# Attention and routed experts on one core: experts with up to 192 tokens get a short branch in which both parts of x pass a weight together

## The chip, the cores and the metric

The kernel runs on one core of a Trainium2 chip. The metric is the device time of one execution in microseconds; the time before is the median of three runs. The profile is one execution taken by the hardware profiler.

## The reference, cut to what matters

First an attention layer: 8 batches, 8 heads, 512 local and 32 global positions, head size 64; local positions attend to a window of 32 on either side and to the global ones, global positions to all. Its output is read as `x`, 4608 tokens of 512. Then a mixture of experts in float32:

```python
do_compute = x @ w_skip > 0
out = x.copy()
xc = x[do_compute]
logits = xc @ w_gate                       # 8 experts
e_idx = np.argmax(logits, axis=1)
gate_w = softmax(logits)[e_idx]
for e in range(8):
    mask = e_idx == e
    h = np.maximum(xc[mask] @ w1[e], 0.0)  # w1: 512 x 1024
    y[mask] = gate_w[mask] * (h @ w2[e])   # w2: 1024 x 512
out[do_compute] = xc + y
```

With the inputs of seed 0 the reference sends 1980 tokens to experts, by expert 395, 171, 153, 289, 173, 371, 253 and 175. The work of each expert depends on its count.

## The kernel before, in words

**Attention and routing** fill the first half. The rows of `out` are written as they come, the router's lists of tokens are scattered into `lst` in DRAM, one list per expert, and the weights of expert 0 are loaded and split alongside.

**The experts** run one after the other from line 969. A group is 256 tokens (`GRP`), in two tiles of 128. GpSimd gathers an expert's first group from `out` into `xfirst` or `xsecond` in turn, and the second group, tokens 256 to 511, into `xmore`; rows beyond the list's end are not moved. `turn_x` (line 832) transposes a group on TensorE and splits it into a rounded part `xh` and the rest `xl`, since TensorE works on rounded float32 (`F32R`). Weights are split likewise: `Weights.split` (line 175) has ScalarE copy a raw chunk of 128 x 1024 to the high part (line 181), and VectorE subtract for the low part (line 184). An expert has eight such chunks of 512 KB, loaded by SP into a ring of six raw buffers (`load`, line 159). The chunks of the next expert are split while the present one computes; the split weights lie in two sets of tiles in turn.

**One group** is done by `ffn` (line 848). The first pass makes the hidden layer in eight blocks f of 128: twelve matmuls of 128 x 256 into one bank `ph` (line 858), four for each of w1h·xh, w1l·xh and w1h·xl; then ScalarE writes the rounded, rectified `hh` (line 863) and VectorE the rest `hlw` (line 864). Three banks serve `ph` in turn. The second pass makes an output tile of 128 tokens by 24 matmuls of 512 columns into `py` (line 874), three for each f: hh·w2h, hh·w2l, hlw·w2h. It runs twice, for t = 0 and 1. `put` (line 936) has VectorE multiply by the gate and add x (line 939), into a buffer `yo` (a pool of two) or `ylast` (one), and GpSimd scatter the rows into `out` (line 940).

**The order of the work around this** is written by hand. All engines record under a manual schedule. `hook(i)` is called behind each block of the first pass (i = 0 to 7), behind each f of the first output tile (8 to 15), and of the second (16 to 23). The table `todo` hangs on it: splits of the next expert's chunks at 0, 1, 2, 4, 5, 6, 9 and 11, and at 16 `nxt`, which loads the expert's count into a register of each engine and turns the next expert's x (`xt`, line 837). Expert 1 also splits the last four chunks of its own weights, at 0 to 3.

**More than 256 tokens** are handled behind the first group under `tc.If(num > GRP)` (line 1010): up to 128 more by `ffn_half` (line 890), otherwise by a further `ffn`. The scatter of the first group's second tile (`leave()`, line 1031) comes last. Each engine tests its own register and jumps.

Of the kernel before, what the change touches and what calls it, by code (L numbers as in the profile page):

```python
# [19 lines left out]
P = 128  # L20
# [14 lines left out]
CAP = NT  # L35
# [4 lines left out]
NSUB = GRP // P  # L40


@with_exitstack
def kernel(
# [59 lines left out]
    def slots(es, g):  # L104
        if g == 0:
            nc.sync.dma_start(
                lt[:, es, 0].rearrange("p e t c -> p e (t c)"),
                l3[es, 0:GRP, :].rearrange("e (p t) c -> p e (t c)", t=NSUB),
            )
        else:  # L110
            for t in range(NSUB):
                nc.sync.dma_start(
                    lt[:, es, 1, t],
                    l3[es, GRP + t * P:GRP + (t + 1) * P, :].rearrange("e p c -> p e c"),
                )
# [22 lines left out]
    wq = {}  # L138

    WC = 1024  # L140

    class Weights:


        def __init__(self, e, pool):
# [5 lines left out]
            self.loaded, self.done, self.n = 0, 0, 2 * NC * F // WC  # L151
# [7 lines left out]
        def load(self, eng=nc.sync):  # L159
            if self.loaded < self.n:  # L160
                i, self.loaded = self.loaded, self.loaded + 1
                raw = self.raw[i] = stage.tile([P, WC], F32, tag="raw", name="raw")
                j = i % (self.n // 2)
                if i < self.n // 2:
                    eng.dma_start(raw, w1[self.e, j * P:(j + 1) * P, :])
                else:
                    k = WC // DM
                    eng.dma_start(
                        raw.rearrange("p (c n) -> p c n", n=DM),
                        w2[self.e, j * k * P:(j + 1) * k * P, :].rearrange(  # L170
                            "(c p) n -> p c n", p=P
                        ),
                    )

        def split(self, eng, parts=1, later=None):
            if self.done < parts * self.n:
# [3 lines left out]
                hi, lo, raw = self.view(i, "h")[:, sl], self.view(i, "l")[:, sl], self.raw[i][:, sl]  # L180
# [639 lines left out]
    stage = ctx.enter_context(tc.tile_pool(name="stage2", bufs=6))  # L820
# [7 lines left out]
    xs = [  # L828
        [f1.tile([P, NC, GRP], F32R, name=f"x{part}{i}") for part in "hl"] for i in range(2)
    ]  # L830

    def turn_x(xg, i, nt=NSUB):
        xh, xl = xs[i]
# [12 lines left out]
        return xh, xl  # L846

    def ffn(e, x2, xg, gate, sidx, hook=lambda i: None, bank=ps_t):
        hl = wq[e]
        xh, xl = x2  # L850
        hh = fw.tile([P, NF, GRP], F32R, name="hh", bufs=1)
        hlw = fw.tile([P, NF, GRP], F32R, name="hlw", bufs=1)
        for f in range(NF):
            ph = ps_s("ph") if bank is ps_v else bank("ph")
            i = 0
            for a, bb in (("w1h", xh), ("w1l", xh), ("w1h", xl)):
                for c in range(NC):
                    nc.tensor.matmul(  # L858
                        ph[:, 0:GRP], hl[a][:, c, f * P:(f + 1) * P], bb[:, c, :],
# [8 lines left out]
            hook(f)  # L868
        for t in range(NSUB):
            py = bank("py")  # L870
            ts_ = slice(t * P, (t + 1) * P)
            for f in range(NF):
                for i, (a, bb) in enumerate(((hh, "w2h"), (hh, "w2l"), (hlw, "w2h"))):
                    nc.tensor.matmul(  # L874
                        py, a[:, f, ts_], hl[bb][:, f, :],
                        start=f == 0 and i == 0, stop=f == NF - 1 and i == 2,
                    )
                hook(NF * (t + 1) + f)

            def leave(t=t, py=py):  # L880
                yo = None
                if t and bank is ps_v:
                    yo = fw.tile([P, DM], F32, name="ylast", bufs=1)
                put(py, gate(t), xg[:, t, :], sidx[:, t:t + 1], yo)

            if t == 0:
                leave()
        return leave

    def ffn_half(e, x2, xg, gate, sidx):  # L890

        hl = wq[e]
        xh, xl = x2
        hh = fw.tile([P, NF, GRP], F32R, name="hh", bufs=1)
# [51 lines left out]
    with tc.manual_schedule(engines=engines | {mybir.EngineType.SP}):  # L946
# [14 lines left out]
        def rest():  # L961
# [4 lines left out]
            for _ in range(4):  # L966
                weights[1].load(nc.gpsimd)
# [126 lines left out]
```

## Time and profile before

| | us |
|---|---|
| median of three runs | 499.26 (497.95 to 500.41) |
| the profiled execution | 503.73 |
| its span, first to last instruction | 502.0 |
| first matmul of expert 0's first pass | 247.6 |
| first matmul of expert 1 | 298.29 |
| first matmul of expert 7 | 469.53 |
| last matmul ends | 491.67 |

The mean granted clock of TensorE is 0.986. HBM traffic is 194 GB/s over the span.

A row of a timeline has start, duration, engine, line, operation, output and inputs, shape, count, and in brackets the idle time of the engine before it with what ended it. PE is TensorE's matmul, PEld its weight load, DVE VectorE, ACT ScalarE, POOL GpSimd, SP the queue that issues most DMAs. A matmul's own duration holds its latency: matmuls overlap, and their pace is read from start to start. A group's row ends in busy time and mean ns of one, and idle time before.

### The profile page before, as it was taken

The page shows a single profiled execution, that of the slowest core. Times are in us where ns is not written, and L with a number is a line of the kernel's source. Part 1 is how long each engine was busy: PE and PEld are TensorE (multiplying, and loading weights), DVE is VectorE, ACT ScalarE, POOL GpSimd, SP SyncE. Part 2 cuts the span into 40 slices and gives each one's busy share as a digit, 9 for nine tenths or more (in the row PEclk, how much of TensorE's full clock was granted, in tenths as well). Part 3 has the DMA queues.
Part 4 walks back from the last instruction along what each step waited for, and adds up shares of the span by engine and source line. Part 5 has one row for each costly group of instructions (what it writes and reads, how often), then busy time and mean ns, then how long its engine had stood idle before and what let it go on. Part 6 is the DMA issues. An engine that isn't in the chain of part 4 may idle for free. (4 is left out here: it accounts for less than half of the span.)

```text
span 502.0 us, 13663 instructions
## 1 busy us (share of the span) xinstructions
PE 455.9 (91%) x4962; PEld 368.5 (73%) x4962; DVE 298.7 (59%) x1221; ACT 289.6 (58%) x883; POOL 228.2 (45%) x236
## 2 busy tenths in 40 slices
PE   8799999999989998887698999999989999899991
PEld 3576767776666767666696979898968888688881
DVE  6886767877757767784453229684714757047310
ACT  4689999899868887764341208563514545145210
POOL 6656666669864677776246014323202341013300
PEclk9999999999999999999899999999999999899996
DMA  8899898889957788610547308883820949113100
GB/s 252 267 329 262 268 288 279 254 281 219 289 171 244 226 189 255 169 45 2 172 146 216 109 26 268 313 295 121 286 99 10 343 142 327 38 23 131 46 15 17
DMA packets 50545, 93.32 MB, mean 186 GB/s; under 512 B 15596, under 2 KB 19948, under 8 KB 50448
## 3 DMA queue, kind: packets, MB, share of 16 engines
q1 hardware_dynamic: 44624, 81.83, 52.0%
q0 software_dynamic: 5824, 10.25, 6.2%
q8 instruction: 55, 0.90, 0.9%
q14 instruction: 42, 0.34, 0.3%
HBM read 82.91 MB, written 14.67 MB: 194 GB/s over the span
## 5 line engine op out<-in xcount | busy, mean ns | idle before, releaser
L368 ACT ACTIVATE prob<-prob,nmx 128x160 f32<-128x160 f32 x256 | 106.4, 418 | 17.9 <-DVE nmx L363 15.7
L398 POOL TENSOR_TENSOR prob<-prob,inv 128x640 f32<-128x640 f32 x64 | 80.3, 1257 | 61.1 <-DVE ing L428 24.0
L863 ACT ACTIVATE hh<-ph 128x256 fp32r<-128x256 f32 x72 | 27.7, 385 | 83.2 <-PE ph L858 71.8
L940 POOL DMA_INDIRECT out_dram<-yo,six x12 | 12.2, 1018 | 134.6 <-DVE yo L939 116.7
L874 PE MATMUL py<-w2h,hh 128*128 128x512 f32 x144 | 57.2, 397 | 0.0
L874 PE MATMUL py<-w2h,hlw 128*128 128x512 f32 x144 | 56.9, 395 | 0.0
L874 PE MATMUL py<-w2l,hh 128*128 128x512 f32 x144 | 56.7, 394 | 0.0
L351 PE MATMUL pss<-ks,qs 64*64 64x160 f32 x1024 | 51.5, 305 | 3.1 <-DVE nmx L363 1.6
L864 DVE SCALAR_TENSOR_TENSOR hlw<-ph,hh 128x256 fp32r<-128x256 f32 x72 | 30.3, 421 | 32.4 <-ACT hh L863 29.6
L351 PEld LDWEIGHTS pss<-ks,qs 64*64 64x64 f32 x1024 | 34.1, 134 | 20.9 <-issue 15.2
L858 PE MATMUL ph<-xh,w1h 128*128 128x256 f32 x288 | 46.4, 283 | 3.2 <-ACT xh L844 1.5
L482 PEld LDWEIGHTS pv<-ptT,vw 128*64 128x64 f32 x1024 | 39.4, 137 | 13.3 <-issue 3.9
L368 ACT ACTIVATION_READ_ACCUMULATOR prob<-prob,nmx 128x1 f32 x256 | 48.4, 189 | 0.0
L482 PE MATMUL pv<-ptT,vw 128*64 128x64 f32 (+1 forms) x1024 | 44.2, 237 | 3.4 <-ACT ptT L441 1.6
L858 PE MATMUL ph<-xh,w1l 128*128 128x256 f32 x288 | 45.5, 280 | 0.0
L858 PE MATMUL ph<-xl,w1h 128*128 128x256 f32 x288 | 45.4, 280 | 0.0
L858 PEld LDWEIGHTS ph<-xh,w1h 128*128 128x128 f32 x288 | 39.3, 191 | 5.9 <-issue 3.8
L639 POOL DMA_INDIRECT lst<-dat,slu x34 | 34.3, 1008 | 18.0 <-DVE cni L959 9.6
L858 PEld LDWEIGHTS ph<-xh,w1l 128*128 128x128 f32 x288 | 39.1, 190 | 0.0
L858 PEld LDWEIGHTS ph<-xl,w1h 128*128 128x128 f32 x288 | 39.0, 190 | 0.0
L438 PE MATMUL pst<-ident,prob 128*128 128x128 f32 x256 | 36.6, 281 | 2.5 <-POOL prob L398 1.2
L184 DVE TENSOR_TENSOR w1l<-raw,w1h 128x1024 fp32r<-128x1024 f32 x28 | 34.1, 1220 | 6.6 <-ACT w1h L181 4.1
(178 smaller groups left out, 942.3 us busy)
## 6 DMA issues: line engine op xcount, KB each, us to landing
raw<-in_w_dram SPq DMA_DIRECT2D x60, 512.0 KB
vw<-in_v_dram SPq DMA_DIRECT2D x32, 512.0 KB
ks<-in_kT_dram SPq DMA_DIRECT2D x32, 400.0 KB
out_dram<-xr SPq DMA_DIRECT2D x32, 256.0 KB
qs<-in_qT_dram SPq DMA_DIRECT2D x31, 256.0 KB
vgs<-in_vgl_dram SPq DMA_DIRECT2D x32, 64.0 KB
raw<-in_w_dram POOLq DMA_DIRECT2D x4, 512.0 KB
lst<-dat,slu POOLq DMA_INDIRECT x34
```

The costliest lines, as they stand in the source:

```text
L184: eng.tensor_sub(lo, raw, hi.bitcast(F32))
L351: nc.tensor.matmul(banks[odd][head(h ^ odd), j * W:(j + 1) * W], q[head(h), w * QB:(w + 1) * QB], window(k[head(h)], w), start=True, stop= ...
L368: nc.scalar.activation(pt[:, i, :], pt[:, i, :], AF.Exp, bias=nmx[:, i:i + 1], scale=-1.0, accum_out=sums[:, i, 0:1],)
L398: nc.gpsimd.tensor_mul(pt[:, sl, :], pt[:, sl, :], inv[:, sl].unsqueeze(2).to_broadcast([P, 4, W]),)
L438: nc.tensor.transpose(pst[:, i * P:(i + 1) * P], pt[:, 4 * hf + i, 0:KW], ident)
L482: nc.tensor.matmul(pv[head(h), j * 96:j * 96 + n], vv[:, w, head(h)], ptT[:, w, h ^ odd, 0:n], start=j == 0, stop=False, skip_group_check= ...
L639: ins = nc.gpsimd.indirect_dma_start(out=lst, out_offset=bass.IndirectOffsetOnAxis(ap=slu[:, t:t + 1], axis=0), in_=dat[:, bs[j], t - 4 * ...
L858: nc.tensor.matmul(ph[:, 0:GRP], hl[a][:, c, f * P:(f + 1) * P], bb[:, c, :], start=i == 0, stop=i == 3 * NC - 1,)
L863: nc.scalar.activation(hh[:, f, :], ph[:, 0:GRP], AF.Relu)
L864: nc.vector.scalar_tensor_tensor(hlw[:, f, :], ph[:, 0:GRP], 0.0, hh[:, f, :].bitcast(F32), ALU.max, ALU.subtract,)
L874: nc.tensor.matmul(py, a[:, f, ts_], hl[bb][:, f, :], start=f == 0 and i == 0, stop=f == NF - 1 and i == 2,)
L940: ins = nc.gpsimd.indirect_dma_start(out=out, out_offset=bass.IndirectOffsetOnAxis(ap=sidx, axis=0), in_=yo, in_offset=None, bounds_check= ...
```

## The change

For experts 1 to 7 the first pass and the second output tile stand in an If with two branches each, on whether the count is over 192 (`FEW`, 128 + 64).

- **The long branch** (`up`, `down`) computes as before, and holds the work on more than 256 tokens (`more`) and the second tile's scatter from `ylast`.
- **The short branch of the first pass** (`up_few`): the two parts of x lie in one tile, so that 2 x 192 columns pass a w1h chunk in one matmul of 384 columns; w1l takes 192 columns of the high part. The bank then holds the high sum beside w1h·xl. ScalarE copies the second half into a `yo` buffer, VectorE adds the first, ScalarE rectifies, VectorE subtracts. The last two follow one block later.
- **The short branch of the second output tile** (`down_few`): `hh` and `hlw` are now one tile `h2`. GpSimd copies the low parts of the last 64 tokens into the columns behind their high parts. Sixteen matmuls with these 128 columns against w2h and w2l make upper and lower halves of `py`, which `leave_few` adds: ScalarE copies the lower half to `ylast`, VectorE takes two steps into a `yo` buffer, and GpSimd scatters 64 rows.
- In the short branch every fourth chunk's subtraction (the third of eight; in expert 1 also the seventh of its own) that falls into the first pass is GpSimd's.
- The first output tile stands between the two Ifs, outside of them.
- `nxt` moves from 16 to 15, ahead of the second If, and loads the next expert's count; expert 1's last splits are at 13 and 14 instead of 13 and 15.
- Weight loads: the raw buffers are six fixed tiles, and SP issues a load behind each split, across experts (`feed`), instead of all eight at the expert's start.
- The lists of experts 1 to 7 are loaded by tile (tokens 0 to 127, then 128 to 255), by two DMAs instead of one, so that tokens 128 to 191 are the first half of the second tile.
- The order of the weights' and x's arithmetic in the long branch, `ffn` for further groups and `ffn_half` stay.

```diff
+Q = P // 2
+FEW = P + Q
...
-        if g == 0:
+        if g == 0 and es.start == 0:
...
-                raw = self.raw[i] = stage.tile([P, WC], F32, tag="raw", name="raw")
...
+                raw = raws[(NCH * (self.e - 1) + i) % len(raws)] if raws else self.raw[i]
...
+    raws.extend(stage.tile([P, WC], F32, name=f"raw{i}") for i in range(6))
...
+    xs = [f1.tile([P, 2, NC, GRP], F32R, name=f"x{i}") for i in range(2)]
+    h2 = f1.tile([P, 2, NF, GRP], F32R, name="h2")
+    hh, hlw = h2[:, 0], h2[:, 1]
...
+    def up_few(e, x2, hook, bank):
+
+        hl, late = wq[e], []
+        for f in range(NF):
+            ph = bank("ph")
+            fs = slice(f * P, (f + 1) * P)
+            for c in range(NC):
+                nc.tensor.matmul(
+                    ph[:, 0:2 * FEW], hl["w1h"][:, c, fs], x2[:, :, c, 0:FEW],
+                    start=c == 0, stop=False, skip_group_check=True,
+                )
+            for c in range(NC):
+                nc.tensor.matmul(
+                    ph[:, 0:FEW], hl["w1l"][:, c, fs], x2[:, 0, c, 0:FEW],
+                    start=False, stop=c == NC - 1, skip_group_check=True,
+                )
+            hs = fw.tile([P, DM], F32, name="yo")[:, 0:FEW]
+            nc.scalar.copy(hs, ph[:, FEW:2 * FEW])
+            nc.vector.tensor_add(hs, ph[:, 0:FEW], hs)
+            if late:
+                late.pop()()
+
+            def part(f=f, hs=hs):
+                h, lo = hh[:, f, 0:FEW], hlw[:, f, 0:FEW]
+                nc.scalar.activation(h, hs, AF.Relu)
+                nc.vector.scalar_tensor_tensor(
+                    lo, hs, 0.0, h.bitcast(F32), ALU.max, ALU.subtract
+                )
+
+            late.append(part)
+            if f == NF - 1:
+                late.pop()()
+            hook(f)
...
+    def down_few(e, hook, bank):
+
+        hl = wq[e]
+        py = bank("py")
+        for f in range(NF):
+            for i, bb in enumerate(("w2h", "w2l")):
+                nc.tensor.matmul(
+                    py, hh[:, f, P:GRP], hl[bb][:, f, :],
+                    start=f == 0 and i == 0, stop=f == NF - 1 and i == 1,
+                )
+            hook(2 * NF + f)
+        return py
...
+    def leave_few(py, xg, gate, sidx):
+        ys = fw.tile([P, DM], F32, name="ylast", bufs=1)
+        nc.scalar.copy(ys[0:Q], py[Q:P])
+        put(py, gate(1), xg[:, 1, :], sidx[:, 1:2], None, ys)
...
-                for _ in range(8 if e else 4):
-                    weights[e + 1].load()
+                for _ in range((4, 2, 0)[min(e, 2)]):
+                    feed()
...
+                    w.split(nc.gpsimd if few and w.done % 4 == 2 else nc.vector)
+                    if e:
+                        feed()
...
+                with tc.If(nums[e] > FEW) as many:
+                    up(e, xs[e % 2], hook, ps_s)
...
+                with many.Else():
+                    up_few(e, xs[e % 2], hook, ps_s)
+                    nc.gpsimd.tensor_copy(hh[:, :, FEW:GRP], hlw[:, :, P:FEW])
+                few = False
+            put(down(e, 0, hook, ps_v), gate(0), xg[:, 0, :], sidx[:, 0:1])
+            if e == 0:
+                second()
+            else:
+                with tc.If(nums[e] > FEW) as many:
+                    second()
+                with many.Else():
+                    leave_few(down_few(e, hook, ps_v), xg, gate, sidx)
```

More of the change, by code (lines that the diff above doesn't have):

```diff
@@ L868, in ffn @@
             hook(f)
-        for t in range(NSUB):
[L870 to L887, printed above, removed]
@@ new lines, in down @@
+    def down(e, t, hook, bank):
+        hl = wq[e]
+        py = bank("py")
+        ts_ = slice(t * P, (t + 1) * P)
+        for f in range(NF):
+            for i, (a, bb) in enumerate(((hh, "w2h"), (hh, "w2l"), (hlw, "w2h"))):
+                nc.tensor.matmul(
+                    py, a[:, f, ts_], hl[bb][:, f, :],
+                    start=f == 0 and i == 0, stop=f == NF - 1 and i == 2,
+                )
+            hook(NF * (t + 1) + f)
+        return py
+    def down_few(e, hook, bank):
+        hl = wq[e]
+        py = bank("py")
+        for f in range(NF):
+            for i, bb in enumerate(("w2h", "w2l")):
+                nc.tensor.matmul(
+                    py, hh[:, f, P:GRP], hl[bb][:, f, :],
+                    start=f == 0 and i == 0, stop=f == NF - 1 and i == 1,
+                )
+            hook(2 * NF + f)
+        return py
@@ L895, in ffn_half @@
-        hlw = fw.tile([P, NF, GRP], F32R, name="hlw", bufs=1)
+        xh, xl = x2[:, 0], x2[:, 1]
         hr = []
@@ L1031, with hook, gate, second @@
-            leave()
-            x2 = x2n[0] if x2n else None
+                todo[15] = nxt
+            def hook(i):
+                todo.get(i, int)()
+            def gate(t):
+                return lt[:, e, 0, t, 1:2]
+            sidx = six[:, e, 0, :]
+            def second():
+                py = down(e, 1, hook, ps_v)
+                with tc.If(nums[e] > GRP):
+                    more(e, nums[e])
+                yl = fw.tile([P, DM], F32, name="ylast", bufs=1)
+                put(py, gate(1), xg[:, 1, :], sidx[:, 1:2], yl)
@@ new lines @@
+            few = False
+            if e == 0:
+                up(e, xs[0], hook, ps_s)
+            else:
+                kept, fed0 = [(w, w.done) for w in weights.values()], fed[0]
+                with tc.If(nums[e] > FEW) as many:
+                    up(e, xs[e % 2], hook, ps_s)
+                for w, w.done in kept:
+                    pass
+                few, fed[0] = True, fed0
+                with many.Else():
+                    up_few(e, xs[e % 2], hook, ps_s)
+                    nc.gpsimd.tensor_copy(hh[:, :, FEW:GRP], hlw[:, :, P:FEW])
+                few = False
```

149 lines of the change are left out of this document (77 added, 72 removed).

## The prediction, made before the run

> **What bounds the kernel now.** I read the page's first part, the busy time of each expert's stretch, and then the timelines of TensorE, ScalarE, VectorE and GpSimd at the seams between experts. The experts are counted from 0; by the token counts given above 1, 2, 4 and 7 have at most 192 tokens; I call them few-experts. First the page (busy us, share, count), then the stretches of experts 1 to 7, each from its first matmul to that of the next (width, then busy us of PE, PEld, DVE, ACT, POOL, then PE clock, DMA share, GB/s).
>
> ```profile
> PE 455.9 (91%) x4962; PEld 368.5 (73%) x4962; DVE 298.7 (59%) x1221; ACT 289.6 (58%) x883; POOL 228.2 (45%) x236
> ```
> ```profile
> 298.29:322.12 23.83, 23.54 (x152) 21.11 (x153) 19.59 (x25) 15.75 (x22) 7.97 (x7) 1.00 0.77 268
> 322.12:345.77 23.65, 23.50 (x152) 20.97 (x153) 14.75 (x21) 11.66 (x18) 7.14 (x6) 1.00 0.70 249
> 345.77:383.18 37.41, 36.01 (x213) 30.83 (x214) 16.86 (x23) 14.26 (x24) 6.98 (x6) 1.00 0.41 137
> 383.18:406.76 23.58, 23.43 (x153) 20.89 (x152) 15.76 (x22) 11.57 (x18) 7.69 (x7) 1.00 0.65 225
> 406.76:445.95 39.19, 37.59 (x212) 31.96 (x213) 16.86 (x23) 14.27 (x24) 6.98 (x6) 0.96 0.41 140
> 445.95:469.53 23.58, 23.43 (x154) 20.90 (x152) 15.67 (x22) 11.45 (x18) 7.10 (x7) 1.00 0.31 95
> 469.53:492.00 22.47, 22.14 (x144) 19.82 (x144) 5.08 (x11) 3.07 (x8) 4.08 (x4) 1.00 0.07 22
> ```
>
> TensorE is busy in all but 0.1 to 1.6 us of each stretch, at full clock: matmuls bound these experts, and a matmul removed is time removed, as long as nothing else becomes late. VectorE is second, with 15 to 20 of 24 us. TensorE's rhythm and two seams without more tokens (expert 1 to 2, and 2 to 3), then the seam behind expert 0, where two jumps follow each other:
>
> ```profile
> 321.43 0.40 PE L874 MATMUL py<-w2h,hlw 128*128 128x512 f32 x1
> 322.12 0.71 PE L858 MATMUL ph<-xh,w1h 128*128 128x256 f32 x4 [0.29 <-PEq L1010]
> ...
> 323.14 0.63 PE L858 MATMUL ph<-xl,w1h 128*128 128x256 f32 x4
> 323.60 0.63 PE L858 MATMUL ph<-xh,w1h 128*128 128x256 f32 x4
> ...
> 339.47 0.39 PE L874 MATMUL py<-w2h,hlw 128*128 128x512 f32 x1
> 339.70 1.04 PE L837 MATMUL xt<-ident,xsecond 128*128 128x128 f32 x8
> 340.49 0.48 PE L874 MATMUL py<-w2h,hh 128*128 128x512 f32 x1
> ...
> 345.23 0.40 PE L874 MATMUL py<-w2h,hlw 128*128 128x512 f32 x1
> 345.77 0.72 PE L858 MATMUL ph<-xh,w1h 128*128 128x256 f32 x4
> ```
> ```profile
> 296.92 0.40 PE L874 MATMUL py<-w2h,hlw 128*128 128x512 f32 x1
> 298.29 0.71 PE L858 MATMUL ph<-xh,w1h 128*128 128x256 f32 x4 [0.97 <-PEq L1016]
> ```
>
> Start to start, four 256-column matmuls take 0.46 to 0.47 us (0.117 each) and one of 512 columns 0.23: 0.456 ns a column. One jump costs 321.43 to 322.12 less 0.23 = 0.46 us, or 0.31 in the last pair of the first fence; I take 0.4. Two in a row cost 296.92 to 298.29 less 0.23 = 1.14.
>
> **The change, part by part.** (1) The first pass of a few-expert. On TensorE, the last output block of a first pass and the start of the second pass, before and after (xh and xl are the parts of x, h_4459 the joint tile of both parts of h):
>
> ```order
> L858 MATMUL ph<-xh_4451,w1h 128x256 x4
> L858 MATMUL ph<-xh_4451,w1l 128x256 x4
> L858 MATMUL ph<-xl_4452,w1h 128x256 x4
> L874 MATMUL py<-w2h,hh 128x512
> L874 MATMUL py<-w2l,hh 128x512
> ```
> ```order
> L883 MATMUL ph<-x_4458,w1h 128x384 x4
> L888 MATMUL ph<-x_4458,w1l 128x192 x4
> L1128 UNCONDITIONAL_BRANCH
> L916 MATMUL py<-w2h,h_4459 128x512
> L916 MATMUL py<-w2l,h_4459 128x512
> ```
>
> In each of eight blocks, twelve matmuls of 256 columns became four of 384 and four of 192. Before: 96 x 0.117 = 11.2 us. After, by columns: 32 x 0.175 + 32 x 0.0875 = 8.4 us. The 192-column ones may not reach 0.0875, since each loads 128 fresh weight columns: the eight transposes above, with 128 moving columns, take 0.79 us, 0.099 each, not 0.058. By that row the pass is 8.8 us; I take 8.8. [...]
>
> (2) The second output tile has 16 instead of 24 matmuls: 5.6 to 3.7 us. TensorE alone then needs 8.8 + 5.6 + 0.8 (transposes) + 3.7 + two jumps of 0.4 = 19.7 us for expert 1, 2 or 4, some 4.0 less than before. For expert 7, which turns no next x, it is 18.5 up to its last matmul, instead of 22.0 (469.53 to 491.5).
>
> (3) ScalarE and VectorE get more to do per block, and the first copy waits for something new. ScalarE at the start of expert 2, before and after (DMASW numbers are the counters of GpSimd's indirect DMAs, gathers and scatters):
>
> ```order
> L863 ACTIVATE hh<-ph 128x256 [waits DVE_49,PE_49,Activation_49]
> L181 CAST w1h<-raw 128x1024 [waits DMAHW1_49]
> L863 ACTIVATE hh<-ph 128x256 [waits PE_49]
> L181 CAST w1h<-raw 128x1024 [waits DMAHW2_49]
> L863 ACTIVATE hh<-ph 128x256 [waits PE_49]
> ```
> ```order
> L893 COPY yo<-ph 128x192 [waits DMASW2_49,DMASW4_49,DMASW1_49,DMASW5_49,DVE_49,DMASW6_49,PE_49,Activation_49]
> L188 CAST w1h<-raw_4451 128x1024 [waits DMAHW1_49]
> L893 COPY yo<-ph 128x192 [waits DMASW4_49,DMASW2_49,DMASW6_49,PE_49,Activation_49]
> L900 ACTIVATE h_4459<-yo 128x192 [waits DVE_49]
> L188 CAST w1h<-raw_4452 128x1024 [waits DMAHW2_49]
> ```
>
> The copy lands in a yo buffer, one of two from which outputs are scattered. So it waits until the last scatter of the expert before has landed. Behind it on ScalarE wait the casts, behind them VectorE's subtractions, and TensorE, with three banks for ph, stops at its fourth block. The prices, from VectorE and ScalarE in expert 2, and from GpSimd at the seams behind experts 0 and 3:
>
> ```profile
> 325.20 1.23 DVE L184 TENSOR_TENSOR w1l<-raw,w1h 128x1024 fp32r<-128x1024 f32 x1 [0.51 <-issue]
> 326.35 0.42 DVE L864 SCALAR_TENSOR_TENSOR hlw<-ph,hh 128x256 fp32r<-128x256 f32 x1
> 326.68 1.22 DVE L184 TENSOR_TENSOR w1l<-raw,w1h 128x1024 fp32r<-128x1024 f32 x1
> ```
> ```profile
> 325.48 1.04 ACT L181 CAST w1h<-raw 128x1024 fp32r<-128x1024 f32 x1
> ```
> ```profile
> 298.38 0.97 POOL L940 DMA_INDIRECT out_dram<-yo,six  x1 [4.51 <-DVEq L1016]
> 300.69 0.97 POOL L940 DMA_INDIRECT out_dram<-ylast,six  x1 [1.33 <-DMA out_dram<-yo,six]
> ...
> 384.47 1.00 POOL L940 DMA_INDIRECT out_dram<-yo,six  x1 [19.96 <-DVE yo L939]
> ```
>
> A weight subtraction holds VectorE 1.15 us, a 256-column step 0.33. I estimate 0.27 for each of the two 192-column steps (by length). A scatter lands about 2.2 us after its start (298.38 to just before 300.69). VectorE has 5 subtractions (the third goes to GpSimd) and 16 short steps in the pass: 5.7 + 4.3 = 10 us. With the first copy and cast ahead of it (0.35 + 1.04) and one more such pair where VectorE runs dry behind the blocks without a subtraction of its own, the last h is ready 12.8 us after the first copy, an estimate from these rows. The end of the expert is then 0.7 + 0.8 + 0.4 + 3.7 later: 18.4 us after the first copy, plus 0.4 to the next, 18.8. The copy can start 1.3 us in at the earliest (a block takes 1.1), and each us beyond is lost.
>
> When can it start? Ahead of expert 2 stands a few-expert. Its end is a copy on ScalarE of half an output, priced by the whole ones in the group below (0.57), two VectorE steps of 0.75 (the row of 491.71 further down), and a scatter:
>
> ```profile
> L549 ACT COPY xr<-pr 128x512 f32<-128x512 f32 x28 | 15.7, 568 | 0.0
> ```
>
> That is 0.8 with the wait for TensorE, + 1.5 + 0.2 + 2.2 = 4.7 us after the last matmul, 4.3 after expert 2 begins. Behind expert 0: 300.6, about 1.6 after a start at 299.0. Behind expert 3: 384.47 + 2.2, 2.4 after a start at 384.3. Behind expert 6 (no more tokens, last yo scatter long landed): no wait.
>
> (4) GpSimd takes one subtraction (two in expert 1) and the copy of h. SP's next weight load waits for that subtraction, and so do all loads behind it.
>
> ```profile
> L184 POOL TENSOR_TENSOR w2l<-raw,w2h 128x512 fp32r<-128x512 f32 x8 | 10.2, 1279 | 0.0
> ```
> ```profile
> 301.96 1.58 POOL L119 DMA_INDIRECT xmore<-out_dram,six  x1 [0.31 <-issue]
> ...
> 306.72 1.16 POOL L119 DMA_INDIRECT xfirst<-out_dram,six  x1 [0.30 <-issue]
> ```
>
> GpSimd's queue at the start of expert 4, before and after:
>
> ```order
> L119 DMA xmore<-out_dram,six 128x512 x2
> L119 DMA xsecond<-out_dram,six 128x512 x2
> L940 DMA out_dram<-yo,six 4352x512
> L982 TENSOR_LOAD cni
> L1010 COMPARE_AND_BRANCH
> ```
> ```order
> L121 DMA xmore<-out_dram,six 128x512 x2
> L121 DMA xsecond<-out_dram,six 128x512 x2
> L1128 COMPARE_AND_BRANCH
> L1128 UNCONDITIONAL_BRANCH
> L191 TENSOR_TENSOR w1l<-raw_4451,w1h 128x1024
> L1135 COPY h_4459<-h_4459 128x8x64
> ```
>
> The subtraction stands behind the four gathers, which end 9.6 us into expert 1, and takes 2 x 1.28 = 2.6. The late casts of expert 1 therefore wait for loads issued at about 12.2; at one 512 KB load in 1.6 to 2 us (268 GB/s in that stretch) the fourth lands at about 19, and behind its cast stand the casts of expert 2's x. So I take 22 us for expert 1, not 1.6 + 18.8 = 20.4. In expert 4 the loads are issued about 12 us in too, but their casts stand in expert 5, 21 us in.
>
> (5) Jumps. A few-expert has one more (counted in 2). Experts 3, 5 and 6 now leave each of their two branches by a jump over the short one: 0.4 inside the expert, and at its end that jump and the next expert's test stand together. Two in a row are 1.14 where experts 3 and 5 had none; a third adds 0.7: 1.8 instead of 0.4 behind expert 6, and 0.7 more behind expert 0. Sum 3 x 0.4 + 2 x 1.14 + 1.4 + 0.7 = 5.6. (6) The end: one copy and one more VectorE step ahead of the last scatter, +0.85, from a VectorE step of 0.75 there. (7) The lists are loaded by four small DMAs, not three; TensorE's 1.35 us wait for the first gather grows by 0 to 0.8, I take 0.4.
>
> ```profile
> 270.81 1.29 PE L837 MATMUL xt<-ident,xsecond 128*128 128x128 f32 x8 [1.35 <-DMA xsecond<-out_dram,six]
> ```
> ```profile
> 491.71 0.75 DVE L939 SCALAR_TENSOR_TENSOR ylast<-py,lt,xsecond 128x512 f32<-128x512 f32 x1 [4.75 <-PE py L874]
> ```
>
> Sum: expert 1 23.8 - 22.0 = 1.8; expert 2 23.65 - (4.3 + 18.8) = 0.5; expert 4 23.6 - (2.4 + 18.8) = 2.4; expert 7 3.5: 8.2 us gained. Less 5.6 + 0.85 + 0.4: **1.35 us net**, 502.4 instead of the 503.73 that the profiled execution took (span 502.0). The median of the three runs is 499.26, and the difference carries over: 497.9, so I say **498**. A measurement can tell about 0.5%, 2.5 us: this would not be told from no change.
>
> **The rivals.** *A, the waits stay hidden*: scatters land sooner or VectorE's steps are shorter, and TensorE keeps its beat. Then experts 1, 2 and 4 gain 4.0 each and 7 gains 3.5; 15.5 - 6.85 = 8.7 us, 490.6 us. For it: VectorE is 18 to 38% idle in these experts now; against it: the copy's wait in the order. *B, slower, by the jumps*: some 13 jumps are new (4 in few-experts, 9 around the others), which I price at 4 x 0.4 + 5.6 = 7.2 us. At the price of the rows below (368.41 to 369.69 less 0.23 = 1.05) they cost 13.7, and the time is 498 + 6.5 = 504.5. It decides above 0.85 us a jump.
>
> ```profile
> 368.41 0.40 PE L874 MATMUL py<-w2h,hlw 128*128 128x512 f32 x1
> 369.69 0.63 PE L837 MATMUL xt<-ident,xmore 128*128 128x128 f32 x4 [0.88 <-issue]
> ```
>
> [...] *C, late loads*: SP's queue, held by GpSimd, makes experts 2 and 4 wait as expert 1 does, 1 to 1.5 us each: 500 to 501.
>
> **How the numbers follow.** The forecast has 0.47: a scatter or a step a little cheaper than taken makes 0.16 of that faster, 0.29 is the same, 0.02 slower. A has 0.22, all faster; B 0.20, of which 0.17 slower and 0.03 the same; C 0.11, of which 0.10 the same and 0.01 slower. Faster 0.38, the same 0.42, slower 0.20. The range reaches from A to B: 490 to 504.
>
> **What would show it.** Right: ScalarE's first copy of expert 2 starts over 4 us after its first matmul and names a scatter; TensorE stops at the fourth block; expert 7 takes 18 to 19 us. Wrong: experts 1, 2 and 4 at 19 to 20 us (A), seams over 2 us with no data wait (B), or casts that wait for raw in expert 4 (C).

## The result, and the profile after

The changed kernel takes 529.08 us (median of four runs, 528.07 to 531.53), the kernel before 498.61 in the same series: 1.062 times as long (95% interval 1.056 to 1.068). That is 30.5 us slower where 1.35 us faster was forecast, and far outside the range. The profiled execution took 528.07 (span 526.4).

The page's busy times show that the arithmetic did shrink: TensorE has 160 matmuls and 2.9 us of work less than before. It is busy 86% of the time, not 91%:

```profile
PE 453.0 (86%) x4802; PEld 364.3 (69%) x4802; DVE 310.6 (59%) x1253; ACT 298.1 (57%) x919; POOL 240.3 (46%) x244
```

The stretches of experts 1 to 7, as shown of before (width, busy time of PE, PEld, DVE, ACT, POOL, then the granted clock, DMA share, GB/s):

```profile
301.76:329.07 27.31, 22.29 (x112) 19.83 (x113) 21.74 (x29) 16.81 (x30) 11.73 (x8) 0.91 0.67 219
329.07:359.67 30.60, 23.79 (x113) 20.29 (x112) 18.22 (x28) 13.62 (x27) 10.52 (x9) 0.89 0.64 210
359.67:396.29 36.62, 36.10 (x213) 31.22 (x212) 17.52 (x24) 15.19 (x25) 6.83 (x6) 1.00 0.40 137
396.29:426.49 30.20, 24.21 (x113) 19.52 (x112) 18.29 (x28) 13.15 (x26) 10.27 (x9) 0.89 0.54 178
426.49:467.43 40.94, 37.74 (x214) 32.23 (x213) 17.52 (x24) 15.18 (x25) 6.27 (x6) 0.96 0.38 132
467.43:493.43 26.00, 23.43 (x153) 20.89 (x152) 16.22 (x22) 11.59 (x18) 8.88 (x9) 1.00 0.28 87
493.43:514.00 20.57, 20.14 (x104) 18.14 (x104) 5.91 (x17) 5.12 (x17) 3.55 (x4) 0.92 0.08 28
```

| stretch (us) | before | after | change | forecast |
|---|---|---|---|---|
| up to expert 1's first matmul | 298.3 | 301.8 | +3.5 | +1.1 |
| expert 1 | 23.8 | 27.3 | +3.5 | -1.8 |
| expert 2 | 23.65 | 30.6 | +7.0 | -0.5 |
| experts 3, 5, 6 together | 100.2 | 103.6 | +3.4 | +4.9 |
| expert 4 | 23.6 | 30.2 | +6.6 | -2.4 |
| expert 7, to the last matmul's end | 22.1 | 20.15 | -2.0 | -3.5 |
| behind the last matmul | 10.3 | 12.8 | +2.5 | +0.85 |

But for rounding, the rows add up to the 24.4 us between the two profiled spans. The 30.5 us are between medians; the profiled execution of the kernel before, 503.73, was itself 5 us over its median.

The sum of the long experts is near the forecast, but by luck. Expert 3 got 0.8 us shorter, 5 and 6 got 1.75 and 2.4 us longer, where 1.5, 1.5 and 1.8 were forecast. No gap stands behind experts 3 and 5, where 1.14 us each was forecast; the time went into a gap inside expert 5 and one behind expert 6. What failed outright are the few-experts and the step into expert 1. TensorE's timeline at expert 2's second If, then at expert 7's:

```profile
350.27 1.05 PE L845 MATMUL xt<-ident,xsecond 128*128 128x128 f32 x8
354.32 0.71 PE L929 MATMUL py<-w2h,h 128*128 128x512 f32 x1 [2.99 <-issue]
354.83 0.63 PE L929 MATMUL py<-w2l,h 128*128 128x512 f32 x1
...
357.39 0.58 PE L929 MATMUL py<-w2l,h 128*128 128x512 f32 x1
357.81 0.39 PE L929 MATMUL py<-w2h,h 128*128 128x512 f32 x1
358.04 0.39 PE L929 MATMUL py<-w2l,h 128*128 128x512 f32 x1
...
509.52 0.39 PE L916 MATMUL py<-w2h,h 128*128 128x512 f32 x1
509.75 0.39 PE L929 MATMUL py<-w2h,h 128*128 128x512 f32 x1
```

In expert 2 TensorE stands still for 2.99 us and no data is named. Then it runs at half speed: 0.43 us from start to start until 357.81 at a granted clock of 0.51, 0.23 afterwards at 1.00. In expert 7 the same jump shows no gap at all. The gaps at this place in experts 1 and 4 are 3.02 and 3.62 us. Others stand ahead of expert 1 (4.68), expert 7 (2.57) and inside expert 5 (2.68).

The prediction did not read the control instructions of a line, the tests and jumps. A row of that view has the instruction, its sequencer (PEldq is TensorE's), how often it ran, then shortest/median/longest ns, and the starts. The test at L1141 in expert 2, then in expert 7; L1128 ahead of expert 1; then, of the kernel before, all of L1010 and that behind expert 1:

```profile
L1141 PEldq COMPARE_BRANCH  x1: 3876/3876/3876, 350.3 to 350.3; - x1
L1141 PEldq COMPARE_BRANCH  x1: 3398/3398/3398, 506.0 to 506.0; - x1
L1128 PEldq COMPARE_BRANCH  x1: 3543/3543/3543, 297.7 to 297.7; - x1
```
```profile
L1010 PEldq COMPARE_BRANCH  x8: 70/3396/4387, 271.5 to 487.4; - x8
L1010 PEldq COMPARE_BRANCH  x1: 4387/4387/4387, 317.6 to 317.6; - x1
```

A jump of TensorE over the code for further tokens takes 3.4 to 4.5 us, and took as long before the change. In that last row it ended at about 322.0, and the next matmul started at 322.12: TensorE's sequencer had come to the jump some 4 us ahead of its matmuls. The 0.46 us that I took for its price was what was left uncovered. In expert 7 the sequencer is 3.8 us ahead (506.0 against 509.75). In expert 2 it is not ahead at all. VectorE's last step, for which the last matmuls of the first output tile wait, ends at 349.70, and the jump starts at 350.3:

```profile
349.34 0.36 DVE L901 SCALAR_TENSOR_TENSOR h<-yo,h 128x192 fp32r<-128x192 f32 x1 [0.16 <-ACT h L900]
```

The code skipped at L1141 is 388 matmuls with their weight loads.

VectorE is late for two reasons. The first was forecast, the copy's wait (4.3 us into expert 2 in the forecast, 5.6 here). The second was not: GpSimd's subtraction beside VectorE's steps. First the scatter, ScalarE's first copy and the subtraction, then VectorE:

```profile
331.80 0.95 POOL L999 DMA_INDIRECT out_dram<-yo,six  x1 [2.08 <-DVE yo L998]
334.67 0.32 ACT L893 COPY yo<-ph 128x192 f32<-128x192 f32 x1 [4.76 <-DMA out_dram<-yo,six]
...
339.76 2.39 POOL L191 TENSOR_TENSOR w1l<-raw,w1h 128x1024 fp32r<-128x1024 f32 x1
```
```profile
339.04 0.35 DVE L901 SCALAR_TENSOR_TENSOR h<-yo,h 128x192 fp32r<-128x192 f32 x1
339.83 0.36 DVE L894 TENSOR_TENSOR yo<-ph,yo 128x192 f32<-128x192 f32 x1 [0.44 <-ACT yo L893]
340.11 2.27 DVE L901 SCALAR_TENSOR_TENSOR h<-yo,h 128x192 fp32r<-128x192 f32 x1
```

While GpSimd subtracts, VectorE's step from two SBUF operands takes 2.27 us instead of 0.35, and ends 0.2 us after GpSimd's. The step that reads ph, in PSUM, is not held (0.36). In the other three places (two in expert 1, one in expert 4) such a step takes 1.76, 2.18 and 2.51 us, and the one from ph 0.36.

The end, on ScalarE, VectorE and GpSimd:

```profile
513.66 0.58 ACT L943 COPY ylast<-py 64x512 f32<-64x512 f32 x1 [8.13 <-PE py L929]
```
```profile
514.34 0.74 DVE L997 SCALAR_TENSOR_TENSOR yo<-py,lt,xsecond 64x512 f32<-64x512 f32 x1 [3.64 <-ACT ylast L943]
515.12 0.74 DVE L998 SCALAR_TENSOR_TENSOR yo<-ylast,lt,yo 64x512 f32<-64x512 f32 x1
```
```profile
516.14 0.92 POOL L999 DMA_INDIRECT out_dram<-yo,six  x1 [4.11 <-DVE yo L998]
```

The last scatter starts 2.56 us after the last matmul's end, before 1.07. The copy, the second step and the waits between them are 1.5 us, not 0.85.

### The profile page after: what moved, and what is told of

It reads as the page before. It is cut to its first block, busy times and chain, and to the rows that moved or that the text cites. A ratio compares the mean times of both kernels' runs of the same rounds, so it can differ in the third digit from the quotient of the medians.

```text
span 526.4 us, 13601 instructions
## 1 busy us (share of the span) xinstructions
PE 453.0 (86%) x4802; PEld 364.3 (69%) x4802; DVE 310.6 (59%) x1253; ACT 298.1 (57%) x919; POOL 240.3 (46%) x244
## 5 line engine op out<-in xcount | busy, mean ns | idle before, releaser
L916 PE MATMUL py<-w2h,h 128*128 128x512 f32 x224 | 73.4, 399 | 1.1 <-DVE h L901 0.9
L916 PEld LDWEIGHTS py<-w2h,h 128*128 128x128 f32 x224 | 41.7, 188 | 12.4 <-DVE h L901 2.1
L864 PE MATMUL ph<-x,w1h 128*128 128x256 f32 x320 | 47.2, 288 | 1.4 <-ACT x L852 1.4
L883 PE MATMUL ph<-x,w1h 128*128 128x384 f32 x128 | 32.5, 381 | 14.1 <-issue 7.2
L864 PEld LDWEIGHTS ph<-x,w1h 128*128 128x128 f32 x320 | 42.8, 196 | 2.3 <-ACT x L852 2.0
L916 PE MATMUL py<-w2l,h 128*128 128x512 f32 x112 | 44.1, 394 | 0.0
L852 ACT CAST x<-xt 128x512 fp32r<-128x512 f32 (+1 forms) x22 | 11.2, 547 | 43.0 <-PE xt L845 40.4
L883 PEld LDWEIGHTS ph<-x,w1h 128*128 128x128 f32 x128 | 24.3, 217 | 16.3 <-issue 8.1
L445 PEld LDWEIGHTS pst<-ident,prob 128*128 128x128 f32 x256 | 27.3, 141 | 10.1 <-issue 5.0
L188 ACT CAST w1h<-raw 128x1024 fp32r<-128x1024 f32 (+1 forms) x36 | 34.1, 947 | 0.3 <-DMA lst<-dat,slu 0.3
L191 DVE TENSOR_TENSOR w2l<-raw,w2h 128x1024 fp32r<-128x1024 f32 x27 | 32.7, 1237 | 2.3 <-ACT w2h L188 2.3
```

The source lines that it names most:

```text
L188: nc.scalar.copy(hi, raw)
L191: eng.tensor_sub(lo, raw, hi.bitcast(F32))
L445: nc.tensor.transpose(pst[:, i * P:(i + 1) * P], pt[:, 4 * hf + i, 0:KW], ident)
L864: nc.tensor.matmul(ph[:, 0:GRP], hl[a][:, c, f * P:(f + 1) * P], x2[:, part, c, :], start=i == 0, stop=i == 3 * NC - 1,)
L883: nc.tensor.matmul(ph[:, 0:2 * FEW], hl["w1h"][:, c, fs], x2[:, :, c, 0:FEW], start=c == 0, stop=False, skip_group_check=True,)
L916: nc.tensor.matmul(py, a[:, f, ts_], hl[bb][:, f, :], start=f == 0 and i == 0, stop=f == NF - 1 and i == 2,)
```

## The experiments

Theory J: the jumps' full length, 3.4 to 4.5 us, shows wherever TensorE's sequencer has no lead, as behind VectorE's late step in experts 1, 2 and 4. The rivals were L (the load of the next count, which the change put right ahead of the test, empties TensorE's queue), W (the waits for data are what costs) and, later, N (a jump costs the same however far it goes). Ratios are against the kernel before, run on the same chip.

**swap2.** The second If with the short branch first. By J the gaps of 3.0, 3.0 and 3.6 us ahead of the short code go, and the far jump stands behind its 16 matmuls:

```diff
-                with tc.If(nums[e] > FEW) as many:
-                    second()
-                with many.Else():
+                with tc.If(nums[e] < FEW + 1) as short:
                     leave_few(down_few(e, hook, ps_v), xg, gate, sidx)
+                with short.Else():
+                    second()
```

> The short branch of the second output tile is recorded first, the long one as its Else; nothing else is changed. [...] With the half clock behind those gaps 6 to 12 us are won: 517 to 523. Theory L (the load of the next count, right ahead of the test, empties TensorE's queue): the gaps stay, 526 to 530. Theory W (the waits for data inside the short branches are what costs, the gaps only show them): 526 to 530 too.

Measured: 512.97 us, 1.032 (1.026 to 1.039), below J's 517 to 523 and far from L and W. The gaps ahead of the second tile are gone. The far jump is still there, 4.79 us from 320.0 in expert 1, now beside the 16 matmuls:

```profile
319.88 0.48 PE L929 MATMUL py<-w2h,h 128*128 128x512 f32 x1
...
325.56 0.76 PE L883 MATMUL ph<-x,w1h 128*128 128x384 f32 x3 [1.75 <-DVE x L853]
```
```profile
L1141 PEldq COMPARE_BRANCH  x2: 73/2434/4794, 318.7 to 320.0; - x2
```

The same work and a jump as long, in another place, are worth some 15 us by the ratios.

**load_early.** The count's load moved here, out of `nxt`:

```diff
             def hook(i):
                 todo.get(i, int)()
+                if i == 8 and 0 < e < E - 1:
+                    numbers(e + 1)
```

> Only the load of the next expert's count is moved, from behind the first output tile to behind its first f (hook 8); the transposes of the next x stay. Theory L: TensorE's queue is full again at the test, the three gaps fall to under 1 us, 517 to 521. Theory J: the load takes 0.3 us of the sequencer and no more, what takes the lead away is the wait for VectorE's last step; at most 1 us is won, 527 to 530. Theory W: no change, 527 to 530.

Measured: 528.88, 1.056 (1.048 to 1.064), no change. The gap in expert 2 is 3.17 us. L falls.

**fixed.** No new Ifs, the branch chosen when the kernel is recorded:

```diff
-                with tc.If(nums[e] > FEW) as many:
-                    second()
-                with many.Else():
+                if e in (1, 2, 4, 7):
                     leave_few(down_few(e, hook, ps_v), xg, gate, sidx)
+                else:
+                    second()
```

(The first If likewise.)

> The two new Ifs are left out: experts 1, 2, 4 and 7 are recorded with the short code, 3, 5 and 6 with the long one, so that which code an expert takes no longer depends on its count when it runs. Theory J: all new jumps are gone and, for the short experts, also the old one; the stretches of experts 1, 2, 4 and 7 fall to 20 to 22 us with the waits for data that the changed kernel shows (2.0, 3.6, 2.2 us): 487 to 493, under the kernel before. Theory W: the waits remain and cost more than the arithmetic saves: 503 or more. Theory L: like J, since no test follows the load; it is told from J by the other runs.

Measured: 501.12, 1.007 (1.004 to 1.011). So 5.5% of the kernel's time, some 27 us, goes with the two Ifs. But J's 487 to 493 is missed: without the tests and jumps the short code is still no faster than the kernel before. The stretches of experts 1, 2, 4 and 7:

```profile
296.84:322.67 25.83, 21.40 (x113) 17.33 (x113) 22.77 (x30) 17.52 (x31) 13.49 (x9) 1.00 0.67 214
322.67:348.57 25.90, 22.71 (x113) 20.45 (x114) 18.34 (x29) 13.24 (x26) 10.02 (x9) 0.87 0.74 235
385.33:408.83 23.50, 20.87 (x113) 17.48 (x112) 18.62 (x28) 13.14 (x26) 9.22 (x8) 1.00 0.59 192
469.18:488.00 18.82, 18.56 (x104) 16.55 (x104) 6.47 (x18) 5.00 (x17) 4.76 (x5) 1.00 0.08 28
```

Expert 7, which has no weights to split, takes the 18.5 us that were forecast. Experts 1, 2 and 4 wait for VectorE. W is right for these, as the smaller part.

**always_long.** Both tests ask for a count over 0:

```diff
-                with tc.If(nums[e] > FEW) as many:
+                with tc.If(nums[e] > 0) as many:
```

> Both new tests ask for a count over 0 instead of over 192, so that every expert takes the long branches; the short code is in the program but never runs. This times the tests and exits alone. Theory J: the tests fall through, the exits jump over 40 to 130 instructions; a gap shows where several jumps follow each other at an expert's end behind the old jump over the further tokens (experts 1, 2, 4, 6, as at the 2.6 us behind expert 6 in the changed kernel, and 4.7 behind expert 0): 500 to 510. Theory L: each second test, right behind the load of a count, costs about 3 us in experts 1 to 6: 515 to 520. Theory W: 498 to 502, the tests are nearly free.

Measured: 511.08, 1.026 (1.020 to 1.032), just above J's range, below L's. No gap over 0.3 us stands at the second tests. What costs are the ends of experts 1 and 2, where exits and the next test follow the far jump, and a gap of 2.82 us inside expert 5 (1.08 before). The first two:

```profile
324.07 1.00 PE L864 MATMUL ph<-x,w1h 128*128 128x256 f32 x4 [2.41 <-PEq L1118]
...
352.03 1.19 PE L864 MATMUL ph<-x,w1h 128*128 128x256 f32 x4 [2.90 <-issue]
```

With the old arithmetic, the rest of the change, tests and exits above all, costs 13.7 us.

**fixed_vec.** Like fixed, all subtractions on VectorE:

```diff
-                    w.split(nc.gpsimd if few and w.done % 4 == 2 else nc.vector)
+                    w.split(nc.vector)
```

> Like fixed (no new Ifs), and the subtractions that the short code gives to GpSimd (one each in experts 2 and 4, two in expert 1) stay on VectorE. Theory G (while GpSimd subtracts, VectorE's step that reads SBUF stands still until it is done: 1.8 to 2.5 us instead of 0.35): VectorE gets 1.15 us of work back for each and loses 1.5 to 2.2 us of standing, so experts 1, 2 and 4 win some 0.5 to 1 us each: 497 to 500. Theory S (what holds the short experts is the first copy's wait for the scatter of the expert before): expert 2 stays as it is, VectorE's extra work makes 1 and 4 up to 1 us longer: 501 to 504.

Measured: 496.46, 0.999 (0.995 to 1.003). By the ratios 0.8% (4 us) less than fixed; G holds and was priced too low. In whole the 192-column steps fall from 512 ns in fixed to 350:

```profile
L901 DVE SCALAR_TENSOR_TENSOR h<-yo,h 128x192 fp32r<-128x192 f32 x32 | 16.3, 512 | 0.5 <-ACT h L900 0.5
```
```profile
L901 DVE SCALAR_TENSOR_TENSOR h<-yo,h 128x192 fp32r<-128x192 f32 x32 | 11.2, 350 | 0.7 <-ACT h L900 0.7
```

**fixed_vec_ys.** Also the last output made in `ylast`:

```diff
-        put(py, gate(1), xg[:, 1, :], sidx[:, 1:2], None, ys)
+        put(py, gate(1), xg[:, 1, :], sidx[:, 1:2], ys, ys)
...
-            nc.vector.scalar_tensor_tensor(yo, py[0:Q], gate, x[0:Q], ALU.mult, ALU.add)
-            nc.vector.scalar_tensor_tensor(yo, rest[0:Q], gate, yo, ALU.mult, ALU.add)
+            nc.vector.scalar_tensor_tensor(yo, rest[0:Q], gate, x[0:Q], ALU.mult, ALU.add)
+            nc.vector.scalar_tensor_tensor(yo, py[0:Q], gate, yo, ALU.mult, ALU.add)
```

> Like fixed_vec, and a short expert's last output is made in the ylast buffer itself and scattered from there, so that the next expert's first copy no longer needs a buffer whose scatter is under way. Only expert 2 follows a short one. Theory S: expert 2 starts its copies some 4 us earlier and is 3 us shorter than in fixed_vec; experts 1 and 4 don't change: 494 to 497 if G holds too, 498 to 501 if not. Theory V (VectorE's own work, about 18.5 us of steps in a short expert, is the bound whatever the copy waits for): at most 1 us less than fixed_vec.

Measured: 494.54, 0.994 (0.991 to 0.996). Expert 2 goes from 24.40 to 22.88 us, experts 1 and 4 stay at 22.8 and 22.7. S is right in kind, and half its size: the second copy still waits, for the first output's scatter.

```profile
323.24 0.32 ACT L893 COPY yo<-ph 128x192 f32<-128x192 f32 x1 [2.84 <-PE ph L888]
...
327.21 0.32 ACT L893 COPY yo<-ph 128x192 f32<-128x192 f32 x1 [2.70 <-DMA out_dram<-yo,six]
```

It is 0.6% faster than the kernel before, but only for counts known when it is recorded.

**merged.** One If per expert, short code first (its Else holds up, the first output tile and second):

```diff
+                with tc.If(nums[e] < FEW + 1) as short:
+                    up_few(e, xs[e % 2], hook, ps_s)
...
+                    put(down(e, 0, hook, ps_v), gate(0), xg[:, 0, :], sidx[:, 0:1])
+                    leave_few(down_few(e, hook, ps_v), xg, gate, sidx)
```

> One If per expert in place of two: both passes of the short code (with its own first output tile) are recorded first, both of the long code as the Else, and the next count is loaded ahead of the If. The arithmetic and the waits for data are those of the changed kernel. Theory J: a short expert has one far jump, behind 16 matmuls without waits (3.7 us), a long one has the far jump at its start, behind the last matmuls of the expert before; little of either shows. So it comes near to fixed (501.1), with 0 to 1 us a seam: 501 to 508. Theory W: what separates the changed kernel from fixed is not the place of the jumps, and it stays over 515.

Measured: 524.71, 1.055 (1.048 to 1.061). The range set for J is missed by 17 us: I had not seen that behind a short expert the jump over the long code and the next, long expert's jump over the short code stand together. Between experts 2 and 3 they are 3.77 and 4.48 us, and TensorE waits 4.79:

```profile
L1132 PEldq COMPARE_BRANCH  x2: 3771/4124/4477, 347.5 to 351.7; - x2
```
```profile
356.35 1.20 PE L864 MATMUL ph<-x,w1h 128*128 128x256 f32 x4 [4.79 <-issue]
```

The rows speak for J (8.2 us of jumps, less the 3.7 us of matmuls), not for W.

**merged_narrow.** Like merged, with fixed_vec's edit, and the short first pass as the long one with 192 columns:

```diff
+            for a, part in (("w1h", 0), ("w1l", 0), ("w1h", 1)):
+                for c in range(NC):
+                    nc.tensor.matmul(
+                        ph[:, 0:FEW], hl[a][:, c, f * P:(f + 1) * P], x2[:, part, c, 0:FEW],
```

> Like merged, but the short first pass is the long one with 192 instead of 256 columns (twelve matmuls a block, ScalarE rectifies, one VectorE step), without the joint passage, the copy and the addition, and with all subtractions on VectorE. By the 192-column matmuls of the changed kernel (0.106 us) TensorE needs 10.2 us for the pass instead of 9.2, but VectorE has one short step a block and nothing waits for a yo buffer. If VectorE and the copy's wait are what eats the gain of the short code (theories G, S and V together): experts 1, 2 and 4 take 20.5 to 21.5 us, expert 7 19.5 to 20: 486 to 493, under the kernel before. If the waits come from something else (late weight loads, ScalarE's casts), they stay and it is no faster than merged.

Measured: 512.07, 1.027 (1.020 to 1.035), 12.6 us less than merged, but over the range, for the same pair of jumps (gaps of 4.10 and 4.43 us ahead of experts 3 and 5).

**short_skip.** The code for more than 384 tokens left out of experts 1 to 7. J, with the distance as the cause of the jumps' length, has 508 to 516, the jumps over the second If's long branch and the gaps under 1 us:

```diff
+            if e == 0:
+                with tc.If(num > GRP + P) as big:
...
+            else:
+                ffn_half(e, turn_x(xmore, e % 2, 1), xmore, gate, sidx)
```

> The changed kernel with the code for more than 384 tokens left out of experts 1 to 7 (a group of 256 and a loop over such groups, some 300 matmuls each that never run with these counts; an expert with more than 384 tokens would come out wrong). What is executed stays the same but for two tests; the long branch of the second output tile shrinks from some 390 matmuls to 84. [...] Rival N (each taken jump, or each test ahead of a jump, costs TensorE the same 3 to 4 us, however far it goes): 525 to 530.

Measured: 508.49, 1.017 (1.010 to 1.023): by the ratios 4.6% (23 us) less than the changed kernel, though what runs is the same but for two tests. The second If's jumps (L1144 here) fall from 3.4 to 4.5 us to at most 0.34:

```profile
L1144 PEldq COMPARE_BRANCH  x10: 70/206/337, 323.5 to 486.8; - x10
L1131 PEldq COMPARE_BRANCH  x10: 70/294/3503, 300.2 to 475.2; - x10
```

The distance matters; N falls. L1131, over the 96 matmuls of the long first pass, still has one of 3.5 us, and the gap ahead of expert 1 is 4.64 us, as it was (4.68).

**swap12_narrow.** Both Ifs short first, with the narrow pass:

```diff
+                with tc.If(nums[e] < FEW + 1) as short:
+                    up_few(e, xs[e % 2], hook, ps_s)
...
+                with short.Else():
+                    up(e, xs[e % 2], hook, ps_s)
```

> Two Ifs as in the changed kernel, both with the short code first; the short first pass is the narrow one of merged_narrow (twelve matmuls of 192 columns a block), all subtractions on VectorE. Theory J: the tests of experts 1 and 7 fall through (their gaps of 4.7 and 2.6 us go, or fall to under 1.5); behind experts 2 and 4 the far jump over the long second tile and the test's jump over the short first pass stand together, as in merged, but the second goes over 96 matmuls only: 2 to 4 us each there. Experts 1, 2, 4 and 7 by themselves at 20.5 to 22: 490 to 500. If the gaps behind 2 and 4 are as in merged_narrow (4.1, 4.4) and the jump over the long first pass shows too: 500 to 508.

Measured: 510.75, 1.023 (1.016 to 1.030), a little over the second case. The gaps ahead of experts 1 and 7 are 1.16 and 0.33 us, those ahead of 3 and 5 are 4.30 and 4.13.

**long_first_narrow.** merged_narrow with the long code first:

```diff
+                with tc.If(nums[e] > FEW) as many:
+                    up(e, xs[e % 2], hook, ps_s)
+                    put(down(e, 0, hook, ps_v), gate(0), xg[:, 0, :], sidx[:, 0:1])
+                    second()
+                with many.Else():
```

> One If per expert as in merged_narrow, but with the long code first. Theory J: no jump stands between a short expert and a long one (the 4.1 and 4.4 us of merged_narrow go); a short expert begins with one far jump over all of the long code, which shows behind expert 0 (no lead, 4 to 5 us), less behind 1 (16 matmuls of lead, 0 to 2 us) and more behind 3 and 6, where the long code's exit stands ahead of it (2 to 5 us each): 497 to 507, 5 to 15 us less than merged_narrow.

Measured: 523.06, 1.048 (1.040 to 1.056), 16 over the range. The gaps ahead of 3 and 5 went as said. Ahead of 1 it waits 5.82 us, ahead of 4 3.04, and ahead of 7 8.21: behind expert 6 three jumps come together, over the code for further tokens, over the short code and over expert 7's long code.

**best.** swap12_narrow, and an expert with more than 384 tokens loops over half groups:

```diff
+                with tc.If(num > GRP + P):
+                    with tc.For_i(GRP + P, num, P) as i:
...
+                        gather(xmore, s2, nt=1)
+                        ffn_half(e, turn_x(xmore, e % 2, 1), xmore, lambda t: lt2[:, t, 1:2], s2)
```

> swap12_narrow (short code first in both Ifs, narrow first pass, all subtractions on VectorE) with the code for more than 384 tokens of experts 1 to 7 made short in another way: such an expert takes a loop of half groups of 128 tokens, which serves any count. The long branch of the second output tile holds some 150 matmuls instead of 390. Theory J: the far jumps over it, 3.9 to 5.3 us in swap12_narrow, shrink, and with them the gaps of 4.3 and 4.1 us behind experts 2 and 4 and the half clock behind those; the test's jump over 96 matmuls may still show there, 0 to 2 us. Experts 1, 2 and 4 take 20.5 to 22 us, 7 takes 20.5: 487 to 495, under the kernel before. If the jump over 150 matmuls costs as much as that over 390: 505 to 511, as swap12_narrow.

Measured: 502.55 against 502.45, 1.001 (0.997 to 1.004), no difference, so the range is missed, though it is 2% better than swap12_narrow by the ratios. The few-experts came close to what was expected (expert 4 a little over); experts 1, 2 and 4:

```profile
301.53:322.38 20.85, 20.85 (x144) 19.14 (x145) 18.17 (x23) 15.14 (x22) 8.22 (x7) 1.00 0.74 271
322.38:344.20 21.82, 21.28 (x145) 18.86 (x143) 16.22 (x23) 12.12 (x20) 10.29 (x8) 1.00 0.86 301
381.22:403.45 22.23, 21.17 (x144) 18.98 (x144) 15.26 (x22) 11.83 (x19) 9.79 (x8) 1.00 0.68 242
```

The jumps over the long second tile (L1138, some 144 matmuls) did shrink: the longest takes 2.99 us, 5.32 in swap12_narrow. Those at L1126, over 96 matmuls of a first pass, still take up to 4.73 us; in swap12_narrow the one ahead of expert 3 took 3.50. The gaps ahead of experts 3 and 5 are only 0.41 and 1.06 us (4.30 and 4.13 there):

```profile
L1138 PEldq COMPARE_BRANCH  x11: 65/229/2994, 316.8 to 480.5; - x11
L1126 PEldq COMPARE_BRANCH  x11: 65/190/4734, 301.1 to 473.4; - x11
```

So the distance alone does not decide how long a jump is: one over 96 matmuls took longer here (4.73 us) than any over 144 (2.99). What else does stays open; that gaps of only 0.41 and 1.06 us show fits J.

In the profiles, from expert 1's first matmul to the last one's end it takes 183.3 us, the kernel before 193.4. It gives back 6 of these 10 us: expert 1 starts at 301.5 instead of 298.3, and 13.1 us follow the last matmul, not 10.3. The other 4 are the difference of the two profiled executions (499.74 and 503.73), which the medians do not show.

**lists_only and best_lists** asked whether the lists by tile take that time: the kernel before with this part alone, and best with the lists that expert 0 needs loaded first:

```diff
-        if g == 0:
+        if g == 0 and es.start == 0:
```
```diff
-            slots(slice(1, E), 0)
-            slots(slice(0, E), 1)
+            slots(slice(1, 2), 0)
+            slots(slice(0, 1), 1)
+            slots(slice(2, E), 0)
+            slots(slice(1, E), 1)
```

> The kernel before with one part of the change alone: the lists of experts 1 to 7 are loaded by tile, by four small DMAs in place of three, with the order of tokens within a group that follows from it. Theory T (this part makes expert 0 longer, where the next x waits for the lists: from expert 0's first matmul to expert 1's first the changed kernel takes 59.2 us and 55.5 without its jump, the kernel before 52.6): 1.5 to 3 us more, 0.3 to 0.6%. Rival: the lists cost nothing, and what differs in expert 0 comes with the other code (the weights' order of loads, expert 0 starting earlier): no change.

> The kernel best with its list loads in another order: the lists that expert 0 itself needs next (expert 1's first group, its own second group) are loaded and turned into indices first, the others behind them. Theory T: expert 0 takes 2 to 4 us less than in best, and the whole is 0.4 to 1% under the kernel before. Rival: expert 0 stays as it is in best, no change against the kernel before.

Measured: lists_only 501.63, 1.004 (1.0005 to 1.007), so 0.2 to 3.7 us for the lists. But its profile doesn't show them where T puts them: from expert 0's first matmul to expert 1's it takes 52.8 us, the kernel before 52.6. (That first matmul stands at 245.73 before; the 247.6 in the table of times further up is a later one.) best_lists: 502.69, 1.005 (1.002 to 1.008), no better than best. T falls as to the place. Expert 1's start, with the gap ahead of it taken off, varies from 294.7 to 300.4 among the profiles of these kernels, whose instructions up to there are almost the same. What moves it stays open.

Over all these runs J gave the direction and the places of the gaps, but its ranges held only in load_early and short_skip: how long a jump would be, and how much of it would show, came out otherwise in the rest.

## Why the prediction was wrong

**The step that failed is (5), the jumps,** and with it rival B's price. I read their cost off TensorE's gaps: 0.46, 0.31, 1.14, 1.05. The first, second and last are what jumps of 4.39, 3.70 and 4.85 us left uncovered in the kernel before; the 1.14 stands at L1016, whose jump took only 0.40 us, and was no price for two far ones. A price per jump is the wrong form. Each costs its length less the sequencer's lead (the one of 4.39 us left a gap of 0.29), and several in a row share one lead (3.77 and 4.48 us left 4.79 in merged). I had 7.2 us for the jumps; fixed puts 27 us on the two Ifs, slower matmuls behind the gaps among them. B (504.5) had the right sign and place, but its 1.05 us a jump was again only such an uncovered rest. The view that would have told, the control instructions of L1010, was in the profile of before.

**Half speed was not in the sum.** "At full clock" was not quite so even in the kernel before: the prediction's own row of expert 5 has 0.96, and behind gaps of 1.08 and 0.52 us there the granted clock is 0.70 from 434 to 438 us. In the changed kernel it is 0.89 to 0.96 in the stretches of experts 1, 2, 4, 5 and 7. swap2 gains some 15 us and closes gaps of 9.6 at the second If; short_skip gains some 23, closes gaps of some 14, and has 1.00 in experts 4, 5 and 7, which fits this.

**(1) and (2) held, with luck:** expert 7 without jumps (fixed) takes 18.56 us, and 18.5 was forecast. But the forecast has 0.4 us for a jump that is not there, and its first pass takes 9.2 us instead of 8.8, since the 192-column matmuls take 0.106 us, not 0.099, and those of 384 columns 0.18, not 0.175. Behind a gap and with half clock at its start it takes 20.15.

**(3) was right in kind.** The first copy of expert 2 waits for the scatter as said, until 1.3 us later, and TensorE stops at the fourth block. What was not seen is that VectorE's late last step also sets when TensorE's sequencer can take the jump.

**(4) failed in its cover.** I let GpSimd's subtraction run beside VectorE and asked only who waits for GpSimd. VectorE stood still under it (1.76 to 2.51 us for a step of 0.35), and fixed_vec puts about 4 us on that. With it gone experts 1 and 4 take 22.8 and 22.7 us: 1.0 and 0.9 us gained instead of 1.8 and 2.4. Its other term, late loads in expert 1 (22 us instead of 20.4), did not come: no cast of expert 1 waits for a load there.

**(6) was too small:** the end cost 1.5 us up to the scatter instead of 0.85; what adds the further 1.0 behind it stays open. **(7) can't be told:** lists_only has 2.0 us (0.2 to 3.7), and the 0.4 of the forecast lies within. A and C did not come: the waits showed, and no cast of expert 4 waited for a load.

## What to carry to other kernels

The gap that a jump leaves is not its cost: read the duration of the test on the engine's sequencer, and count how much queued work, free of late waits, stands ahead of it. Put the rarely run code where a jump over it has matmuls beside it (the 4.79 us of swap2 beside 16), keep two far jumps apart (3.77 and 4.48 us in merged), and keep skipped code short (at the second If 3.4 to 4.5 us over 388 matmuls, at most 0.34 over 84). A short distance is no promise: L1128 jumps over the same 96 matmuls in 3.54 us ahead of expert 1 of the changed kernel and in 0.24 ahead of expert 2. Before work goes to GpSimd, look which of VectorE's steps read two SBUF operands at that time: here they took up to 2.51 us instead of 0.35.

## What the runs showed of the hardware

- At L1010 of the kernel before only TensorE's jumps are long: 3.4 us in the median, on the other engines 0.05 to 0.06. Over 84 matmuls a jump of TensorE took at most 0.34 us (short_skip), over 96 anything from 0.24 (the changed kernel) to 4.7 (best), over 144 at most 3.0 (best), over 388 3.4 to 4.5 (the changed kernel) and up to 5.3 (swap12_narrow).
- Gaps of 2.57 us (ahead of expert 7) and 2.99 us (expert 2) were followed by half clock (a granted clock of 0.50 from 494.5 to 497.5 us and of 0.51 from 354.3 to 357.8; in expert 2 0.43 us for 512 columns), one of 3.02 us in expert 1 was not (1.00 from 325 to 327 us).
- A 192-column matmul took 0.106 us from start to start, a 384-column one 0.18. The joint first pass took 9.2 us (fixed, expert 7), the narrow one with twelve matmuls of 192 columns a block 10.8 (best, expert 7), that of 256 columns 11.0 (the kernel before, expert 7).
